# Another written order for the first batch of a sigmoid-attention and gated-MLP kernel, and the last gate of each first layer on VectorE

## The chip, the cores and the metric

The kernel runs on one core of one Trainium2 chip. The metric is device time in microseconds (us), the median of several executions. A profiled execution gives, beside its own time, the span from the first to the last instruction, and what each engine did in it.

The engines are TensorE (PE in the profile, its weight loads PEld), VectorE (DVE), ScalarE (ACT), GpSimd (POOL, whose queue issues the loads here) and SyncE (SP, whose queue issues the stores). Matmul results lie in PSUM, eight banks of 512 float32 columns in 128 partitions; everything else lies in SBUF.

## The reference

```python
# q, k, v: (8, 12, 448, 64) float32; w_in (768, 2048), w_out (2048, 768), beta (2048)
scores = q @ k.T / sqrt(64) - log(448)
attn   = sigmoid(scores)                 # each element by itself: no row sums
x      = (attn @ v) as (8 * 448, 768)    # the 12 heads side by side
h      = x @ w_in
g      = h * sigmoid(beta * h)
out    = g @ w_out                       # (3584, 768) float32
```

## The kernel before

Matmuls take float16 and sum in float32. One batch (448 tokens, 12 heads) has three *groups* of four heads (g = 0 to 2 for the first batch; `QPB` is 3). For each group:

- `load_one` (L122) issues the load of q or k, or a range of blocks of it, from GpSimd's queue; `load_v` (L143) loads v of one batch in six loads: four of 144 KB for the first 384 keys and two of 48 KB for the last 64, which `double_v_last` (L156) copies to a second place on VectorE.
- `transpose` (L187) turns q and k on VectorE into `qT` and `kT`.
- `visit` or, for the first batch, `half_visit` (L275) does the scores. A half visit takes 224 of the 448 queries and half of the keys (`second` is 0 or 1). Its 16 matmuls (L217) fill two score tiles of two PSUM banks each; then `weigh` (L228) applies the sigmoid on ScalarE, 896 columns at a time (for the last of the four tiles of a group 448).
- `attend` (L293) multiplies the weights with v (L304), for one or both slots of a group (`part`), and copies the result to `xT` on VectorE (L313).

The first layer of the first two batches is `dense1` (L318): for each of 16 columns `dc` of 128 hidden units, six matmuls (L324), a sigmoid on ScalarE (L335) and a multiplication on VectorE (L338). Its loads of w_in come in eight pieces (`load_w_in`, two columns `dc` each). A column can start when all six parts of `xT` for its tokens are there, that is after all three groups. The first batch does it in halves of 224 tokens (`first_batch`, L667), and the order of the pieces of dense work is the generator `early` (L672). `fill_units(n)` takes the next n matmuls off this list.

The start is written out by hand (L697 to L772). `idle_units(n)` issues n matmuls of zeros (L712). Loads are issued in this order: q and k of the three groups (half of q), all of v, the other halves of q, then w_in in eight pieces. TensorE's order is 13 dummies; the six half visits of the first 224 queries with four or two dummies after each of the first five; values and half visits in turns; then dense units between the remaining half visits and values. `share_psum(n)` sets how many score tiles there are (three, later two) and how many banks are left for the rest. ScalarE, VectorE, GpSimd and TensorE each execute their instructions in the order in which they are written.

After the start, a planner hands out dense units between visits by their due times. For each later pair of batches, `blocks` (L495) does the first layer by a Strassen-like scheme: for each of eight blocks i it makes four hidden columns A, D, B and E, each followed by `gate` (L486: sigmoid on ScalarE at L488, product at L491). Gates A, B and D multiply on VectorE; E, whose input lies in SBUF, multiplies on GpSimd. The second layer (`strassen`, L584) takes two row tiles in seven products; the sums of hidden columns that products need come from `hidden_sum` (L578, L582 on VectorE), each asked for about two products ahead. The very last tile goes through `single` and `leave` (L363), which copies a result to SBUF on VectorE (L368) and stores it.

Of the kernel before, what the change touches and what calls it, by code (L numbers as in the profile page):

```python
# [9 lines left out]
FP16 = mybir.dt.float16  # L10
# [3 lines left out]
def kernel(  # L14
# [10 lines left out]
    nc = tc.nc  # L25
# [114 lines left out]
    def last_base(s: int) -> int:  # L140
        return (s % 2 ^ swapped(s // 2)) * KL

    def load_v(b: int):  # L143
        vs[b] = vp.tile([P, H, JF + 1, D], FP16, tag="v16", name="v16")
        rows = v[b].rearrange("h (p c) d -> p h (c d)", c=NB)
        for i in range(HQ):
            nc.gpsimd.dma_start(
                out=vs[b][i * BLK : (i + 1) * BLK, :, 0:JF].rearrange("p h j d -> p h (j d)"),
                in_=rows[:, :, JF * i * D : JF * (i + 1) * D],
            )  # L150
        rows = v[b].rearrange("h (p c) d -> p h c d", c=NB)
        for c in range(NF, NB):
            lo = (c - NF) * BLK
            nc.gpsimd.dma_start(out=vs[b][lo : lo + BLK, :, JF], in_=rows[:, :, c])

    def double_v_last(b: int):  # L156
        nc.vector.tensor_copy(out=vs[b][KL:P, :, JF], in_=vs[b][0:KL, :, JF])

    WCH = 8
    WOUT = 2  # L160

    def load_w_in(c: int):
        n = DFF // WCH
        nc.gpsimd.dma_start(
            out=w_in16[:, :, c * n : (c + 1) * n],
            in_=moe_w_in[:, c * n : (c + 1) * n].rearrange("(c p) f -> p c f", p=P),
        )

    def load_w_out(c: int, half: int):
# [8 lines left out]
    kT = {}  # L178
    at_tiles = {}
    xTs = {}  # L180


    def in_order(b: int, t):
# [3 lines left out]
    def transpose(g: int, r: int, c0: int = 0, c1: int = NB):  # L187
        raw = raws[g][:, r]
        if r == 0:
            if g not in qT:  # L190
                qT[g] = qTp.tile([P, NB * BLK, PAIR], FP16, tag="qT", name="qT")
            nc.vector.transpose(
                out=in_order(g // QPB, qT[g][:, c0 * BLK : c1 * BLK]),
                in_=raw[:, c0:c1].rearrange("p c d -> p (c d)").bitcast(FP32),
            )
            return
        kT[g] = kTp.tile([P, S, PAIR], FP16, tag="kT", name="kT")
        to = kT[g].rearrange("p k e -> p (k e)").bitcast(FP32)
        frm = raw.rearrange("p c d -> p (c d)").bitcast(FP32).rearrange("p (c f) -> p c f", c=NB)
        nc.vector.transpose(  # L200
            out=to[:, 0 : JF * P].rearrange("p (j i q) -> p i j q", j=JF, i=HQ),
            in_=frm[:, 0:NF].rearrange("p (i j) f -> p i j f", j=JF),
        )
        nc.vector.transpose(  # L204
            out=to[:, JF * P :], in_=frm[:, NF:].rearrange("p c f -> p (c f)")
        )
# [6 lines left out]

    def score(sco, u0: int, s: int, jt: int, hh: int, e: int, c0: int, n: int):
        g, lo = s // 2, (s % 2 * 2 + hh) * BLK
        base, nk = (last_base(s), KL) if jt == JF else (0, P)
        nc.tensor.matmul(  # L217
            sco[base : base + nk, hh, u0 : u0 + n],
            kT[g][lo : lo + BLK, jt * P : jt * P + nk, e],
            qT[g][lo : lo + BLK, c0 : c0 + n, e],  # L220
            start=(e == 0),
            stop=(e == PAIR - 1),
            tile_position=(lo, base),
        )
# [50 lines left out]
    def half_visit(g: int, c0: int, second: int):  # L275
        slots = (2 * g, 2 * g + 1)
        scos = [score_tile() for _ in slots]
        plan = [(s, jt, sco, jt * QH) for jt in (0, 1) for s, sco in zip(slots, scos)]
        widths = [S, S]
        if second:  # L280
            plan = [(s, 2, sco, 0) for s, sco in zip(slots, scos)]
            plan += [(s, JF, scos[0], QH) for s in slots]
            widths = [S, QH]
        for i in range(0, len(plan), 2):
            for e in range(PAIR):
                for s, jt, sco, u0 in plan[i : i + 2]:
                    for hh in range(2):
                        score(sco, u0, s, jt, hh, e, c0, QH)
        ats = {id(sco): weigh(sco, n) for sco, n in zip(scos, widths)}
        for s, jt, sco, u0 in plan:  # L290
            at_use(ats[id(sco)], (s, jt, c0), slice(u0, u0 + QH))

    def attend(g: int, c0: int, n: int, part=(0, 1)):  # L293
        b, t = divmod(g, QPB)
        if b not in xTs:
            xTs[b] = xTp.tile([P, NHC, S], FP16, tag="xT", name="xT")
        slots = [2 * g + x for x in part]
        avs = [bank() for _ in slots]
        todo = [(s, av, jt) for s, av in zip(slots, avs) for jt in range(JF)]
# [11 lines left out]
                )  # L311
        for s, av in zip(slots, avs):
            nc.vector.tensor_copy(out=xTs[b][:, s % NPAIR, c0 : c0 + n], in_=av[:, 0:n])  # L313

    gt = const.tile([P, NDC, WIN], FP16, name="gt")
    osbs = {}

    def dense1(b: int, dc: int, hc: int, c0: int = 0, n: int = S):  # L318

        off = (b % 2) * S + c0  # L320
        if hc == 0:
            m2s[b, dc] = bank(n, (b, dc))
        m1 = m2s[b, dc]
# [7 lines left out]
        if hc < NHC - 1:  # L331
            return
        release((b, dc))
        sg = sigp.tile([P, S], FP32, tag="sg", name="sg")
        nc.scalar.activation(  # L335
            out=sg[:, 0:n], in_=m1, func=AF.Sigmoid, bias=0.0, scale=beta_sb[:, dc : dc + 1]
# [26 lines left out]
    def leave(t: int, half: int, m2):  # L363
        lo, hi = half * HALF, (half + 1) * HALF
        release((t, half))
        if t not in osbs:
            osbs[t] = outp.tile([P, DM], FP32, tag="osb", name="osb")
        nc.vector.tensor_copy(out=osbs[t][:, lo:hi], in_=m2)  # L368
        left[t] = left.get(t, 0) + 1
        if t == NT - 1:  # L370
            store(t, lo, hi)
        elif left[t] == 2:
            store(t, 0, DM)
# [121 lines left out]
    def blocks(b: int, other, scores: int):  # L495
# [14 lines left out]
        def whole(key, i):  # L510
            h = kept.pop((i, key))
            if (i, key) in held:
                touch(held.pop((i, key)))
            half, second = {"A": (0, 0), "D": (0, 1), "B": (1, 0), "E": (1, 1)}[key]
            return gate(h, i + half * NB1, b + second, nc.gpsimd if key == "E" else nc.vector)

        for i in range(NB1 + 1):
            p5 = scratch(6 + i % 2, 1).bitcast(FP32)
# [65 lines left out]
    def strassen(t: int, i: int, dc: int):  # L584

        name, x, _, op, w = product(t, i)
        if dc == (0 if i else ND // 2) and i + 2 < NPROD:
            hidden_sum(t, i + 2)
        first = (t, name) not in m2s
        if first:  # L590
# [73 lines left out]
            for dc in range(NDC):  # L664
                yield M2_US, lambda a=(t, half, dc): dense2(*a), False

    def first_batch(c0: int, lo: int, hi: int):  # L667
        for dc in range(lo, hi):
            for hc in range(NHC):
                yield M1_US / 2, lambda a=(0, dc, hc, c0, QH): dense1(*a), False  # L670

    def early():  # L672
        yield from first_batch(0, 0, NDC)
        yield from first_batch(QH, 0, 10)
        yield from plain([(0, 0)])
        yield from first_batch(QH, 10, NDC)
        yield from plain(((1, 0), (2, 0), (0, 1), (1, 1), (2, 1)))

    def second_batch():
        for dc in range(NDC):  # L680
# [17 lines left out]
    with tc.manual_schedule():  # L698
# [12 lines left out]
            for _ in range(n):  # L711
                nc.tensor.matmul(idle, still[:, 0:P], still, start=True, stop=True)  # L712

        idle_units(13)
        for g in range(1, QPB):
            load_one(g, 0, 0, NH)
            load_one(g, 1)
        load_v(0)
        nc.sync.dma_start(out=beta_in[0:NDC], in_=moe_beta.rearrange("(c p) -> c p", p=P))
        for g in range(QPB):  # L720
            load_one(g, 0, NH, NB)
        for c in range(WCH):
            load_w_in(c)
        for g in range(QPB):
            transpose(g, 0, 0, NH)
            transpose(g, 1)

        for g in range(QPB):
            for second in range(2):
                half_visit(g, 0, second)  # L730
                if 2 * g + second < 2 * QPB - 1:
                    idle_units(4 if g < QPB - 1 else 2)
        double_v_last(0)
        transpose(0, 0, NH, NB)
        attend(0, 0, QH, (0,))
        half_visit(0, QH, 0)
        attend(0, 0, QH, (1,))
        attend(1, 0, QH, (0,))
        half_visit(0, QH, 1)
        for g in range(1, QPB):  # L740
            transpose(g, 0, NH, NB)
        attend(1, 0, QH, (1,))
        attend(2, 0, QH, (0,))
        attend(2, 0, QH, (1,))
        half_visit(1, QH, 0)
        for i in range(P // BLK):
            part = slice(i * BLK, (i + 1) * BLK)
            nc.vector.transpose(out=beta_sb[part], in_=beta_in[:, part])
        load_qk(3)
        load_w_out(0, 0)  # L750
        load_w_out(1, 0)
        load_v(1)
        load_qk(4)
        load_qk(5)
        load_w_out(0, 1)
        load_w_out(1, 1)

        share_psum(2)
        fill_units(4 * NHC)
        half_visit(1, QH, 1)  # L760
        attend(0, QH, QH)
        fill_units(3 * NHC)
        half_visit(2, QH, 0)
        fill_units(4 * NHC)
        half_visit(2, QH, 1)
        attend(1, QH, QH)
        fill_units(4 * NHC)
        transpose(QPB, 0)
        fill_units(1 * NHC)
        attend(QPB - 1, QH, QH)  # L770
        transpose(QPB, 1)
        fill_units(4 * NHC)  # L772

        L1B = len(fill)
        fill += list(second_batch())
# [140 lines left out]
```

## Time and profile before

| | us |
|---|---|
| median of 3 executions (381.05 to 381.13) | 381.13 |
| the profiled execution | 381.19 |
| its span, first to last instruction | 379.4 |
| TensorE busy (2927 matmuls) | 370.7 |
| ScalarE busy | 258.4 |
| VectorE busy | 256.8 |
| GpSimd busy | 94.7 |
| L712, 31 dummy matmuls, share of the chain | 2.5% |

The profile's line of a group reads: source line, engine, operation, what it writes and reads with the shape, how often, and in brackets how long the engine had been idle before and what ended that. In a timeline the first number is the start and the second the duration, neighbours of one kind merged. Matmuls are pipelined and their ends are modelled, so that TensorE looks busy also between the starts of two matmuls. The dummies count as busy, too.

### The profile page before, as it was taken

How to read it: one execution, taken by the hardware profiler on the slowest of the kernel's cores; microseconds unless marked ns; L12 is line 12 of the kernel's file. 1: busy time of each engine (PE TensorE's matmuls, PEld its weight loads, DVE VectorE, ACT ScalarE, POOL GpSimd, SP SyncE). 2: the span in 40 equal slices, each digit the busy share in tenths (PEclk: the TensorE clock that was granted, in tenths of full speed). 3: DMA queues.
4: the chain of work that ended last, by engine and by line, in shares of the span. 5: the costliest groups of instructions: out<-in, count | busy, mean ns of one | idle time of the engine just before them, and what ended most of it. 6: DMA issues, size and time to landing. Idle time of an engine off the chain costs nothing.

```text
span 379.4 us, 7379 instructions
## 1 busy us (share of the span) xinstructions
PE 370.7 (98%) x2927; PEld 186.2 (49%) x2927; DVE 256.8 (68%) x483; ACT 258.4 (68%) x303; POOL 94.7 (25%) x141
## 2 busy tenths in 40 slices
PE   8999999999999999999999999999999999999996
PEld 3467664444444455544444445554444445555663
DVE  3256686776687786787576666778667567678662
ACT  3987776688977758887767658887677737882000
POOL 7833353141141012335114003227100002231000
PEclk9999999999999999999999999999999999999999
DMA  7999999993339030009739311007903031000333
GB/s 113 177 187 203 197 205 198 214 126 56 50 54 185 18 83 1 2 2 167 152 65 198 76 44 30 2 0 112 194 0 85 7 78 42 2 0 3 83 83 126
DMA packets 42403, 34.31 MB, mean 90 GB/s; under 512 B 21873, under 2 KB 38913, under 8 KB 42369
## 3 DMA queue, kind: packets, MB, share of 16 engines
q0 software_dynamic: 36976, 22.81, 44.2%
q1 hardware_dynamic: 5392, 11.02, 10.3%
q8 instruction: 23, 0.38, 0.4%
q14 instruction: 12, 0.09, 0.1%
HBM read 45.62 MB, written 11.01 MB: 149 GB/s over the span
## 4 chain that ended last, share of the span: by engine, by line
PE 91%; DVE 5%; ACT 3%; issue 1%; ACTq 0%
PE ps L477 25%; PE ps L593 25%; PE ps L217 12%; PE ps L304 10%; PE ps L324 9%; PE ps L353 4%; PE ps L391 4%; PE ps L712 3%; DVE sum L582 1%; ACT attns L230 1%; DVE xT L313 1%; ACT sg L488 1%; DVE ps L535 1%; DVE w_S L437 1%; DVE gt L491 1%
## 5 line engine op out<-in xcount | busy, mean ns | idle before, releaser
L245 ACT ACTIVATE attns<-ps,nlogs 128x1792 f16<-128x1792 f32 x73 | 128.0, 1753 | 49.3 <-PE ps L217 49.1
L491 POOL TENSOR_TENSOR gt<-attns,sg 128x448 f16<-128x448 f32 x24 | 27.3, 1137 | 151.3 <-ACT sg L488 151.3
L593 PEld LDWEIGHTS <-sum 128*128 128x128 f16 x440 | 39.9, 98 | 38.0 <-issue 11.6
L217 PE MATMUL ps<-qT,kT 32*128 32x448 f16 (+3 forms) x864 | 51.8, 340 | 1.3 <-ACT attns L230 0.6
L488 ACT ACTIVATE sg<-ps,beta_sb 128x448 f32<-128x448 f32 x72 | 45.4, 631 | 8.0 <-PE ps L477 5.8
L593 PE MATMUL ps<-w_T,sum 128*128 128x384 f16 x264 | 49.1, 327 | 0.0
L477 PE MATMUL ps<-xT,w_S 128*128 128x448 f16 x216 | 48.7, 352 | 0.2
L477 PE MATMUL ps<-xT,w_in 128*128 128x448 f16 x216 | 48.7, 353 | 0.0
L313 DVE CAST xT<-ps 128x448 f16<-128x448 f32 (+1 forms) x54 | 28.7, 567 | 27.3 <-PE ps L304 27.2
L491 DVE TENSOR_TENSOR gt<-ps,sg 128x448 f16<-128x448 f32 x72 | 44.6, 619 | 1.4 <-ACT sg L488 1.0
L324 PE MATMUL ps<-xT,w_in 128*128 128x224 f16 (+1 forms) x288 | 40.5, 291 | 1.2 <-ACT attns L230 0.8
L304 PE MATMUL ps<-attns,v 128*64 128x448 f16 (+3 forms) x432 | 41.3, 340 | 0.0
L477 PEld LDWEIGHTS <-w_in 128*128 128x128 f16 x288 | 28.0, 98 | 26.3 <-issue 0.4
L611 DVE TENSOR_TENSOR osb<-ps,osb 128x384 f32<-128x384 f32 x55 | 30.5, 555 | 13.2 <-PE ps L593 11.2
L582 DVE TENSOR_TENSOR sum<-gt 128x1024 f16<-128x1024 f16 x55 | 38.9, 729 | 0.2
L126 POOL DMA_DIRECT2D raw<-in_q_dram x27 | 15.0, 557 | 76.5 <-DVE kT L204 66.7
L593 PE MATMUL ps<-w_out,sum 128*128 128x384 f16 x176 | 32.4, 327 | 1.5 <-DVE sum L582 1.1
L338 DVE TENSOR_TENSOR gt<-ps,sg 128x224 f16<-128x224 f32 (+1 forms) x48 | 21.1, 465 | 18.2 <-ACT sg L335 18.2
L593 PE MATMUL ps<-w_out,gt 128*128 128x384 f16 x176 | 33.3, 327 | 0.0
L324 PEld LDWEIGHTS <-w_in 128*128 128x128 f16 x288 | 26.4, 98 | 14.0 <-issue 6.6
L535 DVE TENSOR_TENSOR ps<-ps,attns 128x448 f32<-128x448 f32 x24 | 15.2, 632 | 24.4 <-PE ps L477 24.4
L477 PEld LDWEIGHTS <-w_S 128*128 128x128 f16 x216 | 21.1, 98 | 20.1 <-issue 0.9
(49 smaller groups left out, 376.0 us busy)
## 6 DMA issues: line engine op xcount, KB each, us to landing
out_dram<-osb SPq DMA_DIRECT2D x98, 96.0 KB, 1.9
raw<-in_k_dram POOLq DMA_DIRECT2D x24, 224.0 KB, 5.4
raw<-in_q_dram POOLq DMA_DIRECT2D x21, 224.0 KB, 4.3
v<-in_v_dram POOLq DMA_DIRECT2D x32, 144.0 KB, 6.9
w_in<-in_moe_w_in_dram POOLq DMA_DIRECT2D x8, 384.0 KB, 10.8
w_out<-in_moe_w_out_dram POOLq DMA_DIRECT2D x4, 768.0 KB, 13.6
v<-in_v_dram POOLq DMA_DIRECT2D x16, 48.0 KB, 6.5
out_dram<-osb SPq DMA_DIRECT2D x2, 384.0 KB, 2.6
```

The source lines that it names most:

```text
L217: nc.tensor.matmul(sco[base : base + nk, hh, u0 : u0 + n], kT[g][lo : lo + BLK, jt * P : jt * P + nk, e], qT[g][lo : lo + BLK, c0 : c0 + n ...
L245: nc.scalar.activation(out=attns[:, slot : slot + 2].rearrange("p n h s -> p (n h) s"), in_=sco, func=AF.Sigmoid, bias=nlogs[:, 0:1], scal ...
L304: nc.tensor.matmul(av[hh * D : (hh + 1) * D, 0:n], vs[b][base : base + nk, 2 * (s % NPAIR) + hh, jt], at[base : base + nk, hh, 0:n], start ...
L313: nc.vector.tensor_copy(out=xTs[b][:, s % NPAIR, c0 : c0 + n], in_=av[:, 0:n])
L324: nc.tensor.matmul(m1, w_in16[:, hc, dc * P : (dc + 1) * P], xTs[b][:, hc, c0 : c0 + n], start=(hc == 0), stop=(hc == NHC - 1),)
L338: nc.vector.tensor_tensor(out=gt[:, dc, off : off + n], in0=m1, in1=sg[:, 0:n], op=ALU.mult)
L477: nc.tensor.matmul(out, w[:, c, i * P : (i + 1) * P], m[:, c], start=(start and c == 0), stop=(c == KH - 1), skip_group_check=not start,)
L488: nc.scalar.activation(out=sg, in_=h, func=AF.Sigmoid, bias=0.0, scale=beta_sb[:, dc : dc + 1])
L491: return lambda: engine.tensor_tensor(out=gt[:, dc, b % 2 * S : b % 2 * S + S], in0=h, in1=sg, op=ALU.mult)
L582: nc.vector.tensor_tensor(out=sums[t, i], in0=x, in1=y, op=op)
L593: nc.tensor.matmul(m2, (x if op is None else sums[t, i])[:, dc], w[:, dc], start=first, stop=(dc == ND - 1), skip_group_check=i >= 4,)
L611: nc.vector.tensor_tensor(out=out, in0=in0, in1=in1, op=op)
```

## The change

1. **Order of the first batch.** 23 dummies in all instead of 31, 11 of them at the very start. v of the first batch is loaded in three groups of four heads (four loads of 48 KB each, then two for the last keys), and the loads come as the list `LOADS` says: v of the first group goes ahead of q and k of the second. w_in comes in five loads of two, two, four, four and four columns. TensorE's order is the list `BEGIN`: values of a group (both slots at once) come between the half visits of other groups, and there are three score tiles until the first 15 dense units are done.
2. **Whole columns.** Of the 16 first dense columns, the first eight stay in halves of 224 tokens; the other eight are done whole, with 448.
3. Two full score tiles of a half visit go through one sigmoid (`weigh_two`, which the kernel had for later batches) where there are two score tiles.
4. The gate E of the last block (i = 7) of each `blocks` multiplies on VectorE instead of GpSimd.
5. `strassen` asks for the first of its hidden sums at the first matmul of a pair of tiles, except in a window's first pair (as before in the middle of the first product).
6. The copy of the last half tile is split: 192 columns on VectorE, 192 on ScalarE.

The rest of the diff is bookkeeping at build time (`ready`, with assertions), which issues no instruction.

```diff
+    def load_v_full(b: int, lo: int = 0, hi: int = H):
...
+        rows = v[b, lo:hi].rearrange("h (p c) d -> p h (c d)", c=NB)
         for i in range(HQ):
             nc.gpsimd.dma_start(
+                out=vs[b][i * BLK : (i + 1) * BLK, lo:hi, 0:JF].rearrange("p h j d -> p h (j d)"),
                 in_=rows[:, :, JF * i * D : JF * (i + 1) * D],
             )
...
+    def load_w_in(lo: int, hi: int):
...
-        ats = {id(sco): weigh(sco, n) for sco, n in zip(scos, widths)}
+        if len(scored) == 2 and not second:
+            two = weigh_two(ps[:, 0:4, 0:S], ())
+            ats = dict(zip(map(id, scos), two if n_sc[0] % 2 == 0 else two[::-1]))
+        else:
+            ats = {id(sco): weigh(sco, n) for sco, n in zip(scos, widths)}
...
+        if t == NT - 1 and half == 0:
+            mid = HALF // 2
+            nc.vector.tensor_copy(out=osbs[t][:, lo : lo + mid], in_=m2[:, 0:mid])
+            nc.scalar.copy(out=osbs[t][:, lo + mid : hi], in_=m2[:, mid:])
...
-            return gate(h, i + half * NB1, b + second, nc.gpsimd if key == "E" else nc.vector)
+            return gate(h, i + half * NB1, b + second, nc.gpsimd if key == "E" and i < NB1 - 1 else nc.vector)
...
-        if dc == (0 if i else ND // 2) and i + 2 < NPROD:
+        if dc == (ND // 2 if i == 0 and t % NTILE == 0 else 0) and i + 2 < NPROD:
             hidden_sum(t, i + 2)
...
+    SPLIT = 8
     def early():
-        yield from first_batch(0, 0, NDC)
-        yield from first_batch(QH, 0, 10)
-        yield from plain([(0, 0)])
-        yield from first_batch(QH, 10, NDC)
-        yield from plain(((1, 0), (2, 0), (0, 1), (1, 1), (2, 1)))
+        yield from first_batch(0, SPLIT, 0, QH)
+        for dc in range(SPLIT, NDC, 2):
+            yield from first_batch(dc, dc + 2)
+            done = (dc - SPLIT) * SPLIT // (NDC - SPLIT)
+            yield from first_batch(done, done + 2 * SPLIT // (NDC - SPLIT), QH, QH)
+        yield from plain(((0, 0), (1, 0), (2, 0), (0, 1), (1, 1), (2, 1)))
...
-        idle_units(13)
+        idle_units(11)
...
+        LOADS = [
+            ("v", 0), ("q", 1, 0), ("k", 1), ("last",), ("q", 0, 1), ("q", 2, 0), ("k", 2), ("v", 1),
+            ("q", 1, 1), ("q", 2, 1), ("v", 2),
+            ("w_in", 0, 2), ("w_in", 2, 4), ("w_in", 4, 8), ("w_in", 8, 12), ("w_in", 12, 16),
+        ]
...
+        BEGIN = [
+            ("q", 0, 0), ("k", 0), ("q", 1, 0), ("k", 1),
+            ("scores", 0, 0, 0), ("idle", 4), ("scores", 0, 0, 1), ("idle", 4),
+            ("v", 0), ("scores", 1, 0, 1), ("q", 2, 0), ("k", 2), ("values", 0, 0),
+            ("scores", 1, 0, 0), ("scores", 2, 0, 0), ("idle", 4), ("scores", 2, 0, 1),
+            ("q", 0, 1), ("q", 1, 1), ("q", 2, 1), ("beta",), ("values", 1, 0),
+            ("scores", 0, 1, 0), ("values", 2, 0), ("scores", 0, 1, 1), ("loads",), ("dense", 12),
+            ("scores", 1, 1, 1), ("dense", 3), ("two",), ("scores", 1, 1, 0), ("values", 0, 1),
+            ("dense", 9), ("scores", 2, 1, 0), ("dense", 18), ("scores", 2, 1, 1),
+            ("values", 1, 1), ("values", 2, 1), ("dense", 24),
+            ("q", 3, 0), ("q", 3, 1), ("k", 3), ("dense", 18),
+        ]
```

In `LOADS`, `("q", g, half)` and `("k", g)` are loads, `("v", n)` is the n-th four heads of v, `("w_in", lo, hi)` a range of columns. In `BEGIN`, q and k are transposes, `("v", 0)` is the doubling copy, `("scores", g, half, second)` a half visit, `("values", g, half)` an `attend` of both slots, `("dense", n)` the next n units, `("loads",)` the later loads (q, k, v, w_out), and `("two",)` the step to two score tiles.

## The prediction

> **What bounds the kernel now.** I read the page's busy line first, then the chain of waits, then the timeline of the first 37 us, and last TensorE's waits over the whole span.
>
> ```profile
> PE 370.7 (98%) x2927; PEld 186.2 (49%) x2927; DVE 256.8 (68%) x483; ACT 258.4 (68%) x303; POOL 94.7 (25%) x141
> ...
> PE 91%; DVE 5%; ACT 3%; issue 1%; ACTq 0%
> ```
>
> TensorE is the bound, so an edit pays only where it removes useless TensorE time or takes work off it. Useless time is nearly all at the front. The chain there:
>
> ```profile
> 1.19 5.73 PE ps L712 x13
> 6.92 0.57 PE ps L217 x13
> 7.49 0.97 PE ps L712 x4
> ...
> 14.32 2.82 ACT attns L230 x3
> ```
>
> L712 are dummy matmuls. PE looks busy, but from 1.2 to 6.85 us it waits for the first q and k, and up to 22 us dummies stand in for work that isn't there. The engine that sets the pace is ScalarE (timeline):
>
> ```profile
> 7.53 13.75 ACT L230 ACTIVATE attns<-ps,nlogs 128x896 f16<-128x896 f32 x16 [4.68 <-PE ps L217]
> ```
>
> It runs without a gap: the starts of successive groups (7.53, 10.93, 14.32) are 3.39 us apart, for a group's two half visits (three sigmoids of 896 columns at 0.905, one of 448 at 0.67). From 24.06 us PE has real work throughout. After that its waits are few (waits, whole span):
>
> ```profile
> PE ps L593 <- DVE sum L582: 1.1, 3, 0.8
> ...
> PE ps L217 <- DVE kT L200: 0.2, 1, 0.2
> ```
>
> The three behind the sums follow the three first layers of batch pairs (0.15, 0.15 and 0.76). The largest:
>
> ```profile
> 344.23 1.13 POOL L491 TENSOR_TENSOR gt<-attns,sg 128x448 f16<-128x448 f32 x1 [3.30 <-ACT sg L488]
> 344.28 2.82 DVE L582 TENSOR_TENSOR sum<-gt 128x1024 f16<-128x1024 f16 x3
> ...
> 345.96 2.77 PE L593 MATMUL ps<-w_out,sum 128*128 128x384 f16 x16 [0.76 <-DVE sum L582]
> ```
>
> The first sum starts beside GpSimd's last gate and takes 1.62 us (maximum of its group) where the median is 0.68: it ends 0.55 after the gate does. PE waits for that one.
>
> **Part 1, the start.** 11 dummies instead of 13 at 0.427 us end at 1.19 + 11 x 0.427 = 5.9. The first kT is written at 6.11 (transposes 5.41 and 5.91), so scores start at 6.2 instead of 6.85, and ScalarE, 0.68 behind, at 6.88 instead of 7.53.
>
> Against this stands the queue on GpSimd: four 48 KB loads of v are issued ahead of group 1's q and k. A v load costs 0.61 to 0.63 us of issue whatever its size (48 KB at L154, 144 KB at L147), so q1 goes out at 5.05 instead of 2.54, k1 at 5.6 instead of 3.06. When does k1 land? What the DMA engines delivered, in slices of 0.4 us from 0:
>
> ```profile
> GB/s 0 0 0 0 0 9 41 65 199 199 211 159 90 92 105 197 190 159 175 148 170 195 166 148 148 169 180 182 189 187 183 169 176 186 191 198 207 136 164 167
> ```
>
> Up to k1 there are now 112+224+192+112+224 = 864 KB (672 before), which this curve reaches at 8.4 us. The first k became usable 0.55 after the curve had its bytes, the next two 1.2 to 1.25 after: k1 at 8.95 to 9.65. I take 9.4; the transposes (0.7, as at 8.52 to 9.22) give kT1 at 10.15. ScalarE has finished group 0 at 6.88 + 3.39 = 10.27, and gets group 1 at 10.2 + 0.68 = 10.88. So it starves 0.6 of the 0.65 us just won.
>
> [...]
>
> From there I follow the written order. The double copy of v, k2's transposes (k2 usable at about 12.7: 1408 KB by the curve at 11.5, plus 1.2) and the xT copies stand in one line on VectorE, and the next four dummies wait for these copies until 14.4; scores (2,0,1) are ready at 16.05, just before ScalarE has done the visit ahead of it (16.1). Values of both slots together cost 0.92 (25.93 to 26.85), one slot alone 0.62 (16.00 to 16.62), so 3 x 0.32 us leave PE, but while ScalarE is late: nothing. On GpSimd 21 issues (twelve of v at 0.62, two of its last part at 0.61, seven of q and k at 0.55) now lie between 2.54 and w_in's first load, which goes out at 15.1 instead of 12.35. With the 2.9 us that k0 took from the end of its issue it lands at 18.8, and the next parts, at 384 KB per 2.0 to 2.2 us as before, at 20.9 and 25.1 (the first eight columns). ScalarE would be held from 20.0 for the first and 26.5 for the third: the cover is a little over 1 us, and beyond it each us of delay costs one.
>
> Up to the last values of the batch, ScalarE must do six group halves and seven gates of 224 columns: 6 x 3.39 + 7 x 0.45 = 23.5, less 0.1 for two pairs of sigmoids in one (1.75 against 1.81). 6.88 + 0.6 + 23.4 = 30.9; the last values end 0.4 later, at 31.3. By then all scores, all values and 42 half-column matmuls of dense are done. The kernel before stands at all scores, all values and 96 such at 37.04 (timeline: values end, L324 restarts). The other 54 cost 54 x 0.1006 (24 in 2.42): 31.3 + 5.4 = 36.7. **-0.3.**
>
> Bounds: k1 at 8.95 gives -0.75, k1 with the 6.35 us that k2 took before (4.10 to 10.45) lands at 11.95 and gives +2.25. The row I use is the curve, since the queue then carries what it carried before.
>
> **Part 2, whole columns.** 48 matmuls of 448 at 0.1977 (13 in 2.57) for 96 of 224 at 0.1006: **-0.17**. ScalarE drops 8 x (2 x 0.45 - 0.63) = 2.2 us and VectorE 8 x (2 x 0.39 - 0.62) = 1.3, behind a PE that is then the bound: nothing, but the 0.21 us that PE waits for a gate at 43.11 may go. Dense 2 of tile 0 moves behind all of the first batch, so w_out has more time.
>
> **Part 3, the gate on VectorE.** In VectorE's order the first sum still precedes the last gate. Without GpSimd beside it the sum ends at 344.28 + 0.68 = 344.96; PE wants it at 345.2. The gate (0.62) then ends at 345.6, the next sum at 346.3; its product starts at 345.2 + 8 x 0.164 = 346.5. All three waits go: **-1.1**. The cover of the next sum is 0.2 us; without it, up to 0.6 at each of three places.
>
> **Part 4, the end.** The last copy takes 0.56 (376.07) and then the store. Two halves side by side: 224 columns take 0.39 on VectorE; ScalarE takes 0.47 for 384. About 0.41: **-0.15** (bounds 0.09 and 0.2).
>
> At nothing: the sum a half product earlier in tiles not divisible by 7 (no PE wait there; 0.68 on VectorE is moved, not added), beta's load and transposes (0.84 on VectorE, idle then), and the bookkeeping in Python.
>
> Sum: -0.3 - 0.17 - 1.1 - 0.15 = -1.7. The profiled execution took 381.19 (span 379.4 and 1.8 around it), 0.06 over the median 381.13: 379.5 for it, **379.4** for the median. A measurement can tell 0.2%, so faster is below 380.4, slower above 381.9.
>
> **Rivals.**
> (a) Slower: group 1 starves ScalarE. If k1 takes 6.35 us from issue to landing, as k2 did, everything to 31.3 slides 2.55: 379.4 + 2.55 = 382.0. It decides from a landing at 11.8. For it: four small loads ahead, and the page's median of 5.4 us for k's loads (11.0, 381.0). Against: the byte curve. Chance 0.18: 0.15 slower, 0.03 same.
> (b) PE stays slow longer. Dummies at 0.427 us up to 6.3 become 0.21 by 7.4: the clock doubles after at least 5 us of steady work. Two fewer dummies leave a hole of 0.3 us before the scores. If the doubling slips past group 0, its visits (0.57, 0.63) and eight dummies (2 x 0.97) take twice as long, 6.3 us, and ScalarE gets its third visit at 13.1 instead of 10.9 (381.6); if it comes midway, half of that: 380.5, which I take. Chance 0.08, same. [...]
> (c) The gate gives its time back: VectorE lags from the 0.62 and the second sum is late by what the first gained: 380.5. Chance 0.06, same.
> (d) A better start: k1 at 8.95 (-0.45) and the waits of 0.21 and 0.2 gone: 378.5. Chance 0.17, faster.
> The forecast has 0.51. Faster 0.51 + 0.17 = 0.68; same 0.17; slower 0.15. The range leaves out most of (a) above and the tail of (d) below: 378.2 to 381.6.
>
> **What would show it.** L712 x11 and first scores at 6.2; ScalarE's first sigmoid at 6.9 with one gap of 0.6 near 10.3; a kT wait on k1 until 9.4; no L491 on GpSimd beside L582 at the three places, no sum of 1.62, and PE without the three waits; the last copy in two engines. Wrong: gaps on ScalarE between 10 and 21 us of over 2 us in all, PE waiting for w_in at the first dense columns, or new PE waits after 40 us.

## The result, and the profile after

380.04 us median (379.51 to 381.89, 22 executions) against 380.94 (380.36 to 381.97, 22): a ratio of 0.9982, 95% interval 0.9974 to 0.9990. The change is faster: by 0.9 us if the medians are taken, by 0.7 (0.4 to 1.0) by the ratio. 1.7 were forecast (379.4 against 381.13). The time lies in the stated range, but the gain is half of what the sum said or less, and the parts of the sum are further off than their total. Their errors have both signs; that the total came this near is luck.

The two lines of the page that answer to those shown before, engines and the chain:

```profile
PE 366.4 (97%) x2871; PEld 181.1 (48%) x2871; DVE 253.8 (67%) x479; ACT 256.5 (68%) x294; POOL 93.2 (25%) x143
...
PE 87%; DMA 4%; POOL 3%; DVE 2%; issue 1%; ACT 1%; ACTq 0%; POOLq 0%
```

TensorE is busy 4.3 us less, yet the span is only 1.2 us shorter (379.4 to 378.2): part of the busy time that went was dummies, and in their place TensorE now waits, for loads (DMA and POOL in the chain, which had none before). TensorE's waits in the changed kernel, us in total, how often, the longest:

```profile
PE ps L236 <- DVE kT L216: 3.3, 4, 1.5
PE ps L350 <- DMA w_in<-in_moe_w_in_dram: 2.3, 3, 1.2
```

The second group is new; the first was one wait of 0.2 us before. The waits behind the hidden sums are gone. The timeline of the start, line by line (L249 is the sigmoid, L216 the larger transpose of k, L236 scores, L177 the loads of w_in, L350 dense columns):

```profile
6.78 3.34 ACT L249 ACTIVATE attns<-ps,nlogs 128x896 f16<-128x896 f32 x4 [3.92 <-PE ps L236]
...
10.42 0.58 DVE L216 STREAM_TRANSPOSE kT<-raw 128x384 f32<-128x384 f32 x1 [0.65 <-DMA raw<-in_k_dram]
...
11.80 10.19 ACT L249 ACTIVATE attns<-ps,nlogs 128x896 f16<-128x896 f32 x12 [1.68 <-PE ps L236]
...
15.34 4.13 POOL L177 DMA_DIRECT2D w_in<-in_moe_w_in_dram  x5
...
20.88 1.32 PE L350 MATMUL ps<-xT,w_in 128*128 128x224 f16 x12 [0.54 <-DMA w_in<-in_moe_w_in_dram]
...
28.27 1.90 PE L350 MATMUL ps<-xT,w_in 128*128 128x224 f16 x18 [1.21 <-DMA w_in<-in_moe_w_in_dram]
```

ScalarE starts at 6.78 as forecast (6.88), then starves 1.68 us for group 1, not 0.6: k1 is usable at 10.4, not 9.4. w_in's first load goes out at 15.34 (forecast 15.1), but its columns are usable at 20.9 and those of the third load at 28.3, not 18.8 and 25.1.

The third first-layer end, where a wait of 0.76 us was:

```profile
343.78 0.69 DVE L614 TENSOR_TENSOR sum<-gt 128x1024 f16<-128x1024 f16 x1
344.39 0.62 DVE L523 TENSOR_TENSOR gt<-attns,sg 128x448 f16<-128x448 f32 x1
344.52 6.29 PEld L625 LDWEIGHTS <-sum 128*128 128x128 f16 x40 [0.22 <-DVE sum L614]
344.53 2.77 PE L625 MATMUL ps<-w_out,sum 128*128 128x384 f16 x16
```

The sum takes 0.69, the gate follows it, and TensorE's product starts with no wait of its own. The tail, where the last copy is split:

```profile
374.63 0.36 DVE L397 COPY osb<-ps 128x192 f32<-128x192 f32 x1 [0.74 <-PE ps L423]
375.03 0.32 ACT L398 COPY osb<-ps 128x192 f32<-128x192 f32 x1 [11.61 <-DVE osb L397]
```

The halves do not run side by side. The second is released by the first, and together they take 0.72 us instead of 0.56. In the program ScalarE's copy waits for a semaphore of VectorE.

Where the time went, from the same places in the two profiled executions (381.19 and 379.93):

| stretch | forecast | measured | from |
|---|---|---|---|
| start, to the end of the batch's values | -0.3 | +1.3 | 32.87 + 54 x 0.1006 = 38.3 against 37.04 |
| from there to the end of the first first layer | -0.17 | -1.1 | last matmuls at 166.35 against 166.19, so +0.16 in all |
| the three places with the gate | -1.1 | -1.6 | +0.16, then -0.14 (254.50), -0.50 (341.80), -1.44 (last copy, 374.63) |
| the split copy | -0.15 | +0.16 | copy done at 375.35 against 376.63 |
| sum | -1.7 | -1.3 | |

These two executions lie 1.26 apart, the medians 0.9: before's was 0.25 over its median, and the changed kernel's 0.11 under. The start also differs between executions: e2 below has the same start, and TensorE stands at the same scores at 38.77 in its trace, at 39.24 in this one.

### The profile page after: what moved, and what is told of

Its sections match the earlier page's. It is cut to its first block, busy times and chain, and to the rows that moved or that the text cites. A ratio compares the mean times of both kernels' runs of the same rounds, so it can differ in the third digit from the quotient of the medians.

```text
span 378.2 us, 7258 instructions
## 1 busy us (share of the span) xinstructions
PE 366.4 (97%) x2871; PEld 181.1 (48%) x2871; DVE 253.8 (67%) x479; ACT 256.5 (68%) x294; POOL 93.2 (25%) x143
## 4 chain that ended last, share of the span: by engine, by line
PE 87%; DMA 4%; POOL 3%; DVE 2%; issue 1%; ACT 1%; ACTq 0%; POOLq 0%
PE ps L625 27%; PE ps L509 25%; PE ps L236 10%; PE ps L328 9%; PE ps L350 8%; PE ps L423 4%; PE ps L380 4%; DMA w_in<-in_moe_w_in_dram 3%; DMA v<-in_v_dram 1%; POOL v L149 1%; POOL raw L126 1%; ACT sg L362 1%; DVE ps L567 1%; DVE gt L365 0%; ACT attns L264 0%
## 5 line engine op out<-in xcount | busy, mean ns | idle before, releaser
L264 ACT ACTIVATE attns<-ps,nlogs 128x1792 f16<-128x1792 f32 x75 | 131.6, 1754 | 50.0 <-PE ps L236 49.9
L523 POOL TENSOR_TENSOR gt<-attns,sg 128x448 f16<-128x448 f32 x21 | 23.9, 1139 | 141.2 <-ACT sg L520 141.2
L236 PE MATMUL ps<-qT,kT 32*128 32x448 f16 (+3 forms) x864 | 52.1, 339 | 4.0 <-DVE kT L216 3.3
L337 DVE CAST xT<-ps 128x448 f16<-128x448 f32 (+1 forms) x54 | 28.3, 566 | 27.6 <-PE ps L328 27.3
L350 PE MATMUL ps<-xT,w_in 128*128 128x448 f16 (+1 forms) x240 | 39.6, 316 | 2.3 <-DMA w_in<-in_moe_w_in_dram 2.3
L509 PEld LDWEIGHTS <-w_in 128*128 128x128 f16 x288 | 28.0, 98 | 26.3 <-issue 0.4
L328 PE MATMUL ps<-attns,v 128*64 128x448 f16 (+3 forms) x432 | 40.5, 340 | 0.0
L614 DVE TENSOR_TENSOR sum<-gt 128x1024 f16<-128x1024 f16 x55 | 36.3, 678 | 0.2
L365 DVE TENSOR_TENSOR gt<-ps,sg 128x448 f16<-128x448 f32 (+1 forms) x40 | 19.7, 526 | 18.8 <-ACT sg L362 18.8
L236 PEld LDWEIGHTS <-kT 32*128 32x128 f16 (+1 forms) x864 | 15.0, 96 | 33.8 <-issue 26.1
L509 PEld LDWEIGHTS <-w_S 128*128 128x128 f16 x216 | 21.1, 98 | 20.1 <-issue 0.9
```

The source lines that it names most:

```text
L236: nc.tensor.matmul(sco[base : base + nk, hh, u0 : u0 + n], kT[g][lo : lo + BLK, jt * P : jt * P + nk, e], qT[g][lo : lo + BLK, c0 : c0 + n ...
L264: nc.scalar.activation(out=attns[:, slot : slot + 2].rearrange("p n h s -> p (n h) s"), in_=sco, func=AF.Sigmoid, bias=nlogs[:, 0:1], scal ...
L328: nc.tensor.matmul(av[hh * D : (hh + 1) * D, 0:n], vs[b][base : base + nk, 2 * (s % NPAIR) + hh, jt], at[base : base + nk, hh, 0:n], start ...
L350: nc.tensor.matmul(m1, w_in16[:, hc, dc * P : (dc + 1) * P], xTs[b][:, hc, c0 : c0 + n], start=(hc == 0), stop=(hc == NHC - 1),)
L365: nc.vector.tensor_tensor(out=gt[:, dc, off : off + n], in0=m1, in1=sg[:, 0:n], op=ALU.mult)
L509: nc.tensor.matmul(out, w[:, c, i * P : (i + 1) * P], m[:, c], start=(start and c == 0), stop=(c == KH - 1), skip_group_check=not start,)
```

## The experiments

**e1, the gate alone.**

```diff
-            return gate(h, i + half * NB1, b + second, nc.gpsimd if key == "E" else nc.vector)
+            return gate(h, i + half * NB1, b + second, nc.gpsimd if key == "E" and i < NB1 - 1 else nc.vector)
```

> The kernel before with one edit alone: the gate of the last block E multiplies on VectorE. If the gate is what pays in the change: the three sums of 1.62 us become 0.68, TensorE's three waits behind L582 (1.1 us in all) go, and the span falls by the 1.4 to 1.6 us that the changed kernel gained after 166 us: about 379.6. Rival, the earlier sums in tiles not divisible by 7 or another part pays: then this kernel gains well under 1 us.

379.25 us against 380.87 on the same chip: 0.9956 (0.9942 to 0.9971). The waits behind the sums are gone, the span is 377.7. The gate alone is worth 1.6 us, more than the whole change. So the other parts together cost 0.8 us by the medians, 1.0 by the ratios.

**e2, no split copy.**

```diff
-        if t == NT - 1 and half == 0:
-            mid = HALF // 2
-            nc.vector.tensor_copy(out=osbs[t][:, lo : lo + mid], in_=m2[:, 0:mid])
-            nc.scalar.copy(out=osbs[t][:, lo + mid : hi], in_=m2[:, mid:])
-        else:
-            nc.vector.tensor_copy(out=osbs[t][:, lo:hi], in_=m2)
+        nc.vector.tensor_copy(out=osbs[t][:, lo:hi], in_=m2)
```

> The changed kernel with the last copy whole again on VectorE. Theory, the two half copies run one after the other (0.36, then 0.32 after a start 0.04 later): the tail is 0.16 us shorter in the trace, about 379.9 against 380.04. Rival, the split does help as forecast: the tail is 0.15 longer.

379.59 us, 0.9969 (0.9959 to 0.9979) of the kernel before. In the trace the tail is one copy of 0.56 from 374.48, the 0.16 us as expected. The difference of the medians to the changed kernel, 0.45, is more than that; the intervals overlap, and only the 0.16 is shown. With the same start as the changed kernel, this trace has k1 usable at 9.8 and a gap of 0.84 us on ScalarE (10.4 and 1.68 there).

**e5, is it the overlap?** The gate as in e1, and the same product on GpSimd once more into a tile that nobody reads.

```diff
+                nc.gpsimd.tensor_tensor(out=still[:, 0:S], in0=h, in1=sg, op=ALU.mult)
                 engine.tensor_tensor(
                     out=gt[:, dc, b % 2 * S : b % 2 * S + S], in0=h, in1=sg, op=ALU.mult
```

> The gate alone, as in e1, and GpSimd does the same product once more at the same moment, into a tile that nobody reads. Theory, the two engines hold each other up when they overlap: the three sums of 0.68 us are 1.62 again and TensorE's waits behind them are back, 1.1 us in all; about 380.7. Rival, the sums were late through the order of work (a dependency on the gate on GpSimd): the sums stay at 0.68 and the time at 379.3.

381.07 us in one execution, and the three waits are back (1.1 us, 3 times, 0.8 the longest). The timeline at the third place:

```profile
344.10 1.13 POOL L493 TENSOR_TENSOR still<-attns,sg 128x448 f16<-128x448 f32 x1 [3.30 <-ACT sg L488]
344.15 1.62 DVE L589 TENSOR_TENSOR sum<-gt 128x1024 f16<-128x1024 f16 x1
...
345.83 2.77 PE L600 MATMUL ps<-w_out,sum 128*128 128x384 f16 x16 [0.77 <-DVE sum L589]
```

Nothing depends on GpSimd's product here, and the sum beside it still takes 1.62 us and ends 0.54 after it. So it is the overlap of the two engines, not the order of work. (This is one execution; the trace carries the argument, not the time.) GpSimd started 0.05 us earlier, and the sum ended 0.54 us after it, a little less than the 0.68 that a sum takes alone (in the changed kernel none of the 55 sums takes more than 0.69). What in the overlap holds the sum up the runs don't show.

**e3 and e4, the loads of the changed start.** e3 loads v of groups 1 and 2 together (four loads of 96 KB for eight of 48 KB); e4 moves q and k of group 1 ahead of v.

```diff
 e3
-                load_v_full(0, a[0] * HQ, (a[0] + 1) * HQ)
+                load_v_full(0, a[0] * HQ, (a[0] + (2 if a[0] else 1)) * HQ)
...
-            ("q", 1, 1), ("q", 2, 1), ("v", 2),
+            ("q", 1, 1), ("q", 2, 1),
 e4
-            ("v", 0), ("q", 1, 0), ("k", 1), ("last",), ("q", 0, 1), ("q", 2, 0), ("k", 2), ("v", 1),
+            ("q", 1, 0), ("k", 1), ("v", 0), ("last",), ("q", 0, 1), ("q", 2, 0), ("k", 2), ("v", 1),
```

> The changed kernel with v of the second and third group in four loads of 96 KB instead of eight of 48 KB. Theory, GpSimd's issue is the bound at the start: w_in's first load goes out about 2 us earlier than 15.34, TensorE's three waits for w_in (2.3 us) shrink to under 0.5, and the kernel is 1 to 2 us faster than the changed one. Rival, the order of TensorE and ScalarE is the bound (ScalarE's gap of 1.7 us near 10): the loads come earlier and the time stays within 0.3 us.

> The changed kernel with q and k of the second group ahead of v of the first in the list of loads; the number of loads is the same. Forecast's step, that v ahead of k costs ScalarE its start: k1 lands at 8.5 as before the change, ScalarE's gap near 10 falls from 1.7 to under 0.3. By the theory that w_in and the number of issues are the bound, TensorE then only waits longer for w_in and the time stays within 0.4 us of the changed kernel; by the rival that the gap of ScalarE is the bound, it falls by 1 us or more.

e3: 380.27 us (0.9978, 0.9963 to 0.9993). Its first w_in load goes out at 12.97, and all waits for w_in are gone, as the theory wanted; the median did not follow. It hides two sorts of executions. The two at a mean granted clock of 0.998 and 1.000 took 378.73 and 378.83, the other eight (0.990 to 0.995) 379.8 to 381.0. The fifteen executions of the changed kernel at 0.998 or more have a median of 379.93, so at full clock the earlier w_in does pay, 1.1 us. The profiled execution of e3 is of the second sort (a line of the timeline; then stretches of 2 us with PE, PEld, DVE, ACT, POOL busy and TensorE's granted clock):

```profile
15.08 0.73 PE L236 MATMUL ps<-qT,kT 32*128 32x224 f16 x16 [2.12 <-DVE kT L216]
...
13.00:15.00 2.00, 0.00 (x0) 0.00 (x0) 0.67 (x3) 1.83 (x2) 1.10 (x2) 1.00 1.44 174
15.00:17.00 2.00, 1.92 (x19) 0.75 (x20) 1.04 (x5) 1.16 (x2) 2.00 (x3) 0.59 1.32 188
17.00:19.00 2.00, 2.00 (x26) 0.74 (x26) 1.51 (x6) 1.04 (x2) 2.00 (x4) 0.56 1.37 180
```

TensorE waits 2.1 us for k2, and then its clock falls: 0.41 and 0.44 of two stretches of 2 us are lost, 1.7 us of full clock, which is 3.4 us at half (a stretch of e9 shows 0.50). Four dummies take 1.86 us instead of 1.04 there. A slow TensorE is what rival (b) of the prediction has, here at another place than the one it named.

e4: 380.13 us (0.9983, 0.9970 to 0.9995), as the changed kernel. k1 does come earlier (its transpose starts at 8.2), but k0, issued at the same moment as ever, comes later (its transpose at 6.34; 5.53 in the changed kernel), ScalarE starts at 7.94, and the first dummies after the scores still run at the slow pace (four in 1.89 us; the next four, at 10.67, take 1.04):

```profile
6.97 0.94 PE L236 MATMUL ps<-qT,kT 32*128 32x224 f16 x16 [0.91 <-DVE kT L216]
...
7.84 1.89 PE L748 MATMUL ps<-still 128*128 128x512 f16 x4
```

Here a hole of 0.9 us ahead of the scores is followed by the slip that rival (b) described. Its profiled execution took 379.96 all the same. Neither single move settles the start. That the order of the loads made k0 late is not shown by one trace: in the other fifteen its transpose begins between 5.3 and 6.0.

**e6, 11 dummies in the old start.** e1 with `idle_units(11)` for `idle_units(13)`.

> The kernel of e1 with 11 dummies instead of 13 at the very start; its loads and its order stay as in the kernel before. Theory, the early start is worth something as long as the loads are not moved: scores at 6.2 and ScalarE's first sigmoid at 6.85 instead of 7.47, no gap on ScalarE up to 20, and 0.6 us less: 378.65. Rival, ScalarE or TensorE then waits for k1, k2 or w_in and gives it back: within 0.2 us of e1.

379.22 us (0.9959, 0.9944 to 0.9974), as e1. k0 was usable only at 5.88 in its trace, the scores began at 6.51 (6.86 in e1), ScalarE has no gap up to 21, and the span is 0.2 shorter. The early start is kept, but it is bounded by k0, whose transpose begins anywhere between 5.3 and 6.0 in all traces but e4's; what is left is too small to be seen in four executions.

**e7 and e8, each half of the new start alone.** e7: the order of TensorE as before, the new list of loads, the gate. e8: the new order, with the loads as before.

```diff
 e8
-            ("v", 0), ("q", 1, 0), ("k", 1), ("last",), ("q", 0, 1), ("q", 2, 0), ("k", 2), ("v", 1),
-            ("q", 1, 1), ("q", 2, 1), ("v", 2),
-            ("w_in", 0, 2), ("w_in", 2, 4), ("w_in", 4, 8), ("w_in", 8, 12), ("w_in", 12, 16),
+            ("q", 1, 0), ("k", 1), ("q", 2, 0), ("k", 2), ("v", 0), ("last",),
+            ("q", 0, 1), ("q", 1, 1), ("q", 2, 1),
+            *(("w_in", c, c + 2) for c in range(0, 16, 2)),
```

> The kernel of e1 (order of TensorE as before, 13 dummies) with the changed kernel's loads: v by head groups, the first ahead of q and k of group 1, w_in in five loads. Theory, the loads are what the changed start pays for: k1 is usable at 10.4 instead of 8.5, k2 at 13.4 instead of 10.5, ScalarE starves 2 to 3 us before 15 and TensorE reaches dense 1.5 to 2.5 us late: 380.8 to 381.8. Rival, the loads are neutral and the order of TensorE's work is what costs: within 0.4 us of e1.

> The kernel of e2 (changed, whole last copy) with the loads as before the change: q and k of all groups, then v in four loads of 144 KB, w_in in eight. Theory, order and loads belong together: k1 comes at 8.5, but the values of group 0 stand third in TensorE's order and wait for v until about 14.5, so ScalarE starves 2 us there and the time is 0.5 to 1.5 us above e2. Rival, the loads alone were the loss: 0.5 us or more below e2.

e7: 381.86 us, 1.0027 (1.0017 to 1.0037): 2.6 us over e1. ScalarE's gap before group 1 is 1.46, and TensorE waits 1.7 us for w_in. e8: 383.08, 1.0061 (1.0046 to 1.0077): 3.5 us over e2, more than expected. TensorE's longest wait in e8 is the one foreseen:

```profile
PE ps L328 <- DMA v<-in_v_dram: 2.6, 1, 2.6
```

The mean granted clock in its four executions is 0.987 to 0.990; 0.013 of 378 us would be 4.9 us of full clock, some of it lost while TensorE waited anyway. How the 3.5 us divide between the wait and the clock is not separated. Loads and order belong together; each alone is worse than either start.

**e9 to e11, another order for both.** q and k of all groups first, then v; both half visits of group 1 ahead of the values of group 0. e9 has v of groups 1 and 2 in four loads, e10 in eight, e11 all of v in four.

```diff
+            ("q", 1, 0), ("k", 1), ("q", 2, 0), ("k", 2), ("v", 0), ("last",), ("q", 0, 1),
+            ("v", 1), ("q", 1, 1), ("q", 2, 1),
...
+            ("scores", 1, 0, 1), ("scores", 1, 0, 0), ("v", 0), ("values", 0, 0),
+            ("scores", 2, 0, 0), ("idle", 4), ("scores", 2, 0, 1),
```

> The kernel of e2 with loads and order matched: q and k of all three groups first, then v of group 0 (four loads of 48 KB), the last keys, v of groups 1 and 2 together (four of 96 KB), w_in in the five loads; in TensorE's order both half visits of group 1 stand ahead of the values of group 0. Theory, the start is worth time only if every load is there when its place in the order comes: k1 at 8.5, k2 at 10.5, w_in's first load issued at 12.5 to 13, ScalarE without a gap over 0.3 from 6.9 to 20, dense from about 19; 1 to 2 us below e2, 377.6 to 378.6. Rival, the DMA engines are the bound whatever the order: k, v or w_in come late elsewhere and the time is within 0.4 us of e2.

> As e9, with v of groups 1 and 2 in eight loads of 48 KB, so four issues more ahead of w_in. Theory, the number of issues on GpSimd sets when w_in comes: its first load goes out about 2 us later than in e9, TensorE waits 1 to 2 us more for w_in: 0.7 to 1.7 us above e9. Rival, the DMA engines are the bound: same time as e9.

> As e9, with all of v in four loads of 144 KB as in the kernel before: four issues fewer, but v of group 0 is usable only with the rest, at about 14. Theory of head groups, early values need early v: TensorE waits 2 us for v at the values of group 0, ScalarE starves behind it, 1 to 2 us above e9. Rival, the fewer issues outweigh it: as e9 or faster.

e9 381.22, e10 382.25, e11 380.63: none better than e2, against the theory of e9. The mean granted clock is under 0.998 in 7 of 12, 4 of 4 and 9 of 10 executions. In e9 k1 and k2 do come at 8.6 and 10.4 and ScalarE runs from 10.6 to 17.4; then TensorE waits for v of group 1 (1.2 us) and for copies that stand behind the late q on VectorE (1.1), and the clock falls (granted clock 0.68 from 18 to 21 us and 0.50 from 21 to 24). e10 is 1.0 us over e9, as the theory of issues said, but by the same waits and not by w_in. In e11 TensorE does wait 2.0 us for v, as expected, but the time is not 1 to 2 us above e9: 0.9992 (0.9980 to 1.0004) against 0.9998 (0.9983 to 1.0013), the same within what they resolve. e10 is at 1.0049 (1.0034 to 1.0064).

**e12 to e14, dummies in the gaps.** e12: the changed kernel with nine more dummies where TensorE waits anyway. e13: the same for e3 with 13, and the last copy whole. e14: e13 with k2 moved up. In all three the transposes of q and k of group 2 also move behind the values of group 0.

```diff
 e13 (e12: 10 and 3, e14: 9 and 5)
-            ("scores", 0, 0, 0), ("idle", 4), ("scores", 0, 0, 1), ("idle", 4),
-            ("v", 0), ("scores", 1, 0, 1), ("q", 2, 0), ("k", 2), ("values", 0, 0),
-            ("scores", 1, 0, 0), ("scores", 2, 0, 0), ("idle", 4), ("scores", 2, 0, 1),
+            ("scores", 0, 0, 0), ("idle", 4), ("scores", 0, 0, 1), ("idle", 9),
+            ("v", 0), ("scores", 1, 0, 1), ("values", 0, 0), ("q", 2, 0), ("k", 2),
+            ("scores", 1, 0, 0), ("idle", 8), ("scores", 2, 0, 0), ("idle", 4), ("scores", 2, 0, 1),
```

> The changed kernel with nine dummies more in gaps where TensorE waits anyway (six ahead of the first scores of group 1, three ahead of those of group 2; the transposes of q2 and k2 stand behind the copies of the values on VectorE, so that the dummies' bank is free). Theory, TensorE's clock halves for some us in part of the executions, because the changed start has fewer dummies: with them the mean granted clock is 0.998 or more in every execution, and the median is 0.1 to 0.3 below the changed kernel's. Rival, the lower clock has another cause: it is 0.99 to 0.996 in a quarter or more of the executions, as before, and the time does not move or rises.

> The kernel of e3 (v of groups 1 and 2 in four loads) with the last copy whole and 13 more dummies in its two gaps (five and eight). In e3 the two executions at full clock took 378.8 and the eight at 0.99 to 0.995 took 379.8 to 381.0. Theory, the clock took what the earlier w_in gave: full clock in every execution and 378.4 to 378.9. Rival, the lower clock follows from something else: 0.99 to 0.995 in most executions and 380 or more.

> As e13, with q and k of group 2 ahead of the last keys of v in the list of loads, and five instead of eight dummies in the second gap. Theory, what is left of the start is the wait for k2: it lands 1 us or more earlier than in e13 and the time falls by 0.3 to 1.0. Rival, the last keys, now later, hold the values of group 0 and with them the scores behind: as e13 or slower.

| kernel | median | ratio to before (95%) | mean granted clock under 0.998 |
|---|---|---|---|
| before | 380.94 | | in none of the 23 beside e1, nor beside e9 or e12 |
| changed | 380.04 | 0.9982 (0.9974 to 0.9990) | 7 of 22 |
| e12 | 379.72 | 0.9979 (0.9965 to 0.9993) | 1 of 12 |
| e3 | 380.27 | 0.9978 (0.9963 to 0.9993) | 8 of 10 |
| e13 | 378.89 | 0.9948 (0.9936 to 0.9960) | 0 of 5 |
| e14 | 379.62 | 0.9975 (0.9963 to 0.9986) | 3 of 12 |
| e1 | 379.25 | 0.9956 (0.9942 to 0.9971) | 0 of 4 |

Against e3, e13 keeps its clock (0 of 5 executions under 0.998 against 8 of 10), and the earlier w_in then pays: 378.89 us is the lowest median of all, 1.9 us under the kernel before beside it. Its interval overlaps that of e1, the gate alone, so that it beats the old start is not shown. Its gaps, filled (timeline):

```profile
8.51 2.12 PE L743 MATMUL ps<-still 128*128 128x512 f16 x9
...
13.39 1.89 PE L743 MATMUL ps<-still 128*128 128x512 f16 x8
```

e12 (1 of 12 against 7 of 22 of the changed kernel) points the same way less clearly. It gains 0.3 us in the median, which its interval doesn't separate from the changed kernel; two of its 12 executions took 381.6 and 381.7, one of them at full clock, and the cause of that is open. e14's rival holds: the last keys come late and TensorE waits 0.9 us for them.

## Why the prediction was right and wrong

**Part 3, the gate: right in mechanism, 0.5 us too small.** The three waits are gone, and e1 and e5 show why. The sum counted TensorE's waits as the profile lists them (0.15, 0.15, 0.76). The traces gained 0.30, 0.36 and 0.94: a listed wait begins at the modelled end of the matmul before it, which is later than the moment when the next could have started. At the third place (the kernel before, then the changed one):

```profile
342.76 2.44 PE L593 MATMUL ps<-w_out,gt 128*128 128x384 f16 x14
...
342.25 2.44 PE L625 MATMUL ps<-w_out,gt 128*128 128x384 f16 x14
```

In the changed kernel the next product starts 2.28 us after the first of these 14, at 344.53. Before, that would have been 345.04, and it started at 345.96: 0.92 late.

**Part 1, the start: wrong, and the step that failed is when the loads land.** For k1 the row taken was "the curve, since the queue then carries what it carried before". It does not. The delivered rate of the changed kernel, in slices of 0.4 us from 0:

```profile
GB/s 0 0 0 0 0 10 33 96 173 197 206 167 137 113 139 107 98 95 77 152 160 140 146 158 174 173 164 175 189 179 185 165 130 120 115 180 206 138 86 119
```

From 6.0 to 7.6 us it is 77 to 107 GB/s where the curve of before had 159 to 197, and from 12.8 it falls to 115 to 130 while small loads of v are issued. The bytes up to k1 are there at 9.2, not 8.4, and the delay of 1.2 behind them was right. It is not this execution alone: in the seven traces with the same loads up to k1 its transpose begins at 9.8 to 10.4, never at the forecast's 9.4. ScalarE had group 1 at 11.80 instead of 10.88.

For w_in the row taken was k0's, 2.9 us from the end of its issue; but k0 is the second load of all. The traces have nearer rows, those of w_in itself (the kernel before, then the changed one):

```profile
DMA to landing us min/median/max: 6.0/10.8/15.0
...
DMA to landing us min/median/max: 5.5/11.2/17.7
```

The minimum is the first load. With its 6.0 us from before, an issue at 15.1 lands at 21.1; it was usable at 20.9, and 18.8 was forecast. So the cover of "a little over 1 us" was gone: the 2.3 us of waits. Of the 1.6 us by which the last values are later than forecast (32.87 against 31.3), 0.9 is there at group 1 already, and the rest arises later, where TensorE waits for w_in. From 15 to 20 us the table of stretches has 120 GB/s (164 before). Why the rate is lower the runs don't separate: loads of 48 KB follow each other at 0.55 us or more on GpSimd, 90 GB/s at most, and the short rows of v's last keys are moved earlier. e3 and e7 show the cost from both sides: with four issues fewer the waits for w_in go, and the new loads under the old order cost 2.6 us.

**Part 2, whole columns: too small.** The stretch after the start gained 1.1 us, not 0.17, and nearly all of it in the dense columns of the first batch: with all of them done, and the first four visits of the next batch, the 17th matmul of the second layer starts at 52.16 before and at 52.20 after, so the 1.3 us lost at the start are made up by then. The price of the matmuls was about right: between starts they are 0.096 and 0.189 us apart, which gives 0.14 in place of the 0.17. What the sum put at nothing is time in which TensorE stood still in the kernel before:

```profile
37.28 0.67 DVE L313 CAST xT<-ps 128x224 f16<-128x224 f32 x2
37.71 0.10 PEld L324 LDWEIGHTS <-w_in 128*128 128x128 f16 x1 [0.27 <-issue]
...
38.01 1.72 PEld L324 LDWEIGHTS <-w_in 128*128 128x128 f16 x18 [0.20 <-issue]
...
43.11 0.48 PEld L324 LDWEIGHTS <-w_in 128*128 128x128 f16 x5 [0.38 <-issue]
```

By the gaps of the weight loads that is 0.27, 0.20 and 0.38 us, 0.85 in all: two waits for banks that the copies to xT free, and one behind a gate. The prediction knew only the last, as "0.21 us" that "may go". From 32.87 on, the changed kernel has no such wait in its columns. Whether whole columns did that, with fewer gates, or the new order, in which the copies come at another place, is not separated: part 2 was not run alone.

**Part 4, the split: wrong sign.** Side by side was assumed; the copies run in turn, and e2 has the 0.16 us back.

**The rivals.** (a) k1 took 5.1 us from issue, between the forecast's 3.8 and the rival's 6.35; a k1 later than the curve has it is 0.9 of the 1.6 us by which the start was missed. (b) is the clock, at 0.08. The changed kernel's trace shows no slip at the place that it named. The prediction has the clock double after at least 5 us of work; here the dummies are 0.43 us apart only up to 4.55, 3.4 us after the first, and 0.22 from there, so that the 11 of them end at 5.4 and the hole before the scores is 0.8 us, not 0.3, without harm. Yet 7 of the 22 executions lost clock: their median is 380.63, where that of the other fifteen is 379.93. Where they lost it no trace shows; in e3 it is behind the wait for k2. The mean clocks group near 1.000, 0.995, 0.991 and 0.987. One fall to half for T us costs T / 2 of 378: 0.0045 is T = 3.4 us, and the groups are none, one, two and three times that. The traces agree with these steps: by their stretches the time at half is about 3.4 us in e3, e10 and e11 and 6.8 in e9, at mean clocks of 0.995, 0.996, 0.995 and 0.991. A wait of 2.1 us, with scores and values on TensorE right up to it, was enough in e3. (c) did not happen: the next sum was ready in time at all three places. (d) needed k1 at 8.95, and no trace with these loads has it before 9.8.

## What to carry to other kernels

A dummy matmul in a gap is not waste if it holds the clock (with 13 more of them no execution of e13 is under 0.998, where 8 of 10 of e3 are): before taking one out, ask what keeps TensorE busy in that gap in the worst execution, and look at the mean granted clock of every execution, not at one profile. An instruction whose longest duration is over twice its median (1.62 us against 0.68), beside another engine's, was the cheapest find in this profile: one line, moved to the engine that it disturbed, gave 1.6 us. An order of work and an order of loads are one design: e7 and e8 each took half of a pair and lost 2.6 and 3.5 us. And the time from issue to landing of a load is best taken from a load that stood in the same place of the queue, not from the first one: w_in's first load took 6.0 us before the change, where the forecast, from k0, had 3.7.

## What the runs showed of the hardware

- k0 is issued at 1.94 or 1.95 us in all sixteen traces, and its transpose begins at 5.3 to 6.0 us, in e4 at 6.34. k1, with the same loads up to it, is usable at 9.8 to 10.4. So a start read from one execution is uncertain by half a microsecond.
- On GpSimd's queue a load of w_in costs 0.83 to 0.88 us of issue for 384 KB, and 768 KB cost no more (0.85 to 0.87 in the changed kernel, five in 4.13).
- The clock fell although TensorE was not idle all the time before. In e3 and e9 to e11 TensorE was busy for about 1.0 to 1.6 of the 3.4 us ahead of the fall (e3: 1.3 us from 11.95 to 15.36). In the changed kernel's trace the least busy stretches of 3.41 us between 4.5 and 372 us have 1.86 us (one is 7.93 to 11.34), and the clock stayed. Where the line lies is not shown: at the end of that trace, 1.44 us from 373.16 to 376.57 was not followed by a fall either.
- Two copies from one PSUM bank on two engines ran one after the other as the program has them, 0.36 and 0.32 us for 192 columns each, 0.04 apart.
